# One planned order for the first batch's mixing, and third forms on VectorE, in an RWKV-6 and MLP-mixer kernel

## The chip, the core and the metric

The kernel runs on one core of a Trainium2 chip. The metric is the device time of one execution in microseconds (us). Before the change the median of three runs is 520.51 us (519.77 to 521.84). Five engines work side by side, each on its own queue in order: TensorE (PE; its weight loads are shown as PEld), VectorE (DVE), ScalarE (ACT), GpSimd (POOL) and SyncE (SP), which issues nearly all DMAs here.

## The reference

Four batches, eight heads, 768 tokens, 48 values per head. First a linear attention with a decaying state, then a mixer over tokens and one over channels:

```python
for t in range(S):                                  # attention, per batch and head
    cur = u[:, None] * (k_t outer v_t)
    y[t] = r_t @ (state + cur)
    state = w_t[:, None] * state + (k_t outer v_t)
x = y as (B, 768, 384)
h = relu(x.T @ w_tok1) @ w_tok2                     # 768 -> 256 -> 768 over tokens
u = x + h.T
out = u + relu(u @ w_ch1) @ w_ch2                   # 384 -> 1536 -> 384 over channels
```

The mixer's weights arrive as 64-bit floats and are turned into 32-bit floats on the chip.

## The kernel before

**Attention** is done in twelve units, three per batch (`UB = 3`), each for 256 tokens of a batch; `unit(i)` returns its steps. In the order of their dependence: `ends` (a scan on DVE, L392, and a reciprocal), `keys` (L397), `begins` (a scan, L400), `queries` (L403), `tokens` (transposes on PE, L307) with two copies on ACT (`copied`, L308), `carry` (PE, L323), four pairs of `scaled` on ACT (L458) and `updates` on DVE (L468) that follow each other, `gram` (PE, L277) and `mask` (DVE), `before` (the across product on PE, L337, which needs the fourth `scaled`), `seen` (a small read on ACT, L349), `after` (the within product on PE, L358) and three copies `taken` into x (ACT, L364). Units 0 to 3 compute the term with u by a gram of its own (`own_u` on ACT, `own_gram`, `own_put`); later units by three products on DVE (L420, L422, L425; in the code `products`, the buffer `near`). Two range checks on ACT (`ranges`, L384) read each unit's `to_end`, a buffer that the next unit's `ends` overwrites. `load_rk`, `load_w`, `load_v` and `load_near` issue the loads of the next unit on SP.

**Conversion** of weights goes by pairs of blocks: two loads (L226), on DVE `exponent` (L229), `mantissa` (L235), `add` (L241) and `put` (L244 and two of L247), on ACT `raise_two` (L232) and `signs` (L238). The token weights take three pairs, the channel weights nine (`to_ch`, pairs 0 to 8): `w_ch1` lies in pairs 0 to 4 and `w_ch2` in 4 to 8.

**Mixing of batch 0** is done in 32-bit float: `hidden` (L774), `back` (L781, an addition into x on DVE), `turn` (L789, transposes; a copy on ACT), `up` (L799; three steps and a ReLU on ACT, L802), `down` (L810) for two of three thirds of the tokens (each 12 blocks of hidden channels, `jt`), and `quarters` for the last third: seven products p1 to p7 (L829, L834) of sums of blocks, for which `weight_sum` forms sums of weights on DVE (L764). Blocks `jt` 0 to 3 of `up` need pairs 0 and 1, 4 to 7 pairs 1 and 2, 8 to 11 pairs 3 and 4; of `down`, 0 to 3 need pairs 4 and 5, 4 to 7 pairs 6 and 7, 8 to 11 pairs 7 and 8.

**Mixing of batches 1 to 3** (`exact_mixing`) splits both factors in parts of fewer bits. For the weights `splits(kind, n)` makes three forms, six times for each of the two kinds: up part (ACT, L528), remainder (DVE, L532), low part (ACT, L536), a store of the low part to DRAM (SP, L542 or L544), and the third form "joint" (POOL, L547), the difference of up and low part. Each block then takes `joint` (L624), `ends` (L647, L649), sums and forms of z on ACT, DVE and POOL, and `down` (L661 to L663); the stored low parts come back through a ring of ten slots (`load_third`, L563).

**Order.** `strict` ties the instructions of PE, DVE, ACT and SP to the order in which they are recorded. The attention of batch b + 1 runs beside the mixing of batch b. Up to unit 2 the order is written out by hand. For batch 0's mixing the program has a hand-written list (`ahead`) and then `woven`, which merges lists in proportion to rough weights: conversions with ups, then the rest. For batches 1 and 2 `interleaved` plans: each piece lists its engines, their times and the pieces that it needs, and a small model of the engines' clocks and of the six PSUM banks decides whether the next piece of mixing or of attention is recorded. Batch 1's forms of the second kind (`late`) are set in by hand, two steps at a piece.

```python
pieces = woven(first, woven(both[2:], sum(to_ch[2:8], [])) + woven(downs[0][:4], to_ch[8]))
...
pieces += woven([(0.4, f) for f in e2["ranges"]] + second + sum((a + b for a, b in rest), []), mixed)
```

Of the kernel before, what the change touches and what calls it, by code (L numbers as in the profile page):

```python
# [21 lines left out]
DM = H * D  # L22
# [27 lines left out]

def woven(*lists):

    keyed = []
    for n, pieces in enumerate(lists):
        total, at = sum(c for c, _ in pieces), 0.0
        for i, (c, f) in enumerate(pieces):
            keyed.append(((at + c / 2) / total, n, i, c, f))
            at += c
    return [(c, f) for *_, c, f in sorted(keyed, key=lambda e: e[:3])]


def emit(pieces):
    for _, f in pieces:
        f()
# [3 lines left out]
def rwkv6_then_mixer(  # L68
# [456 lines left out]
    def splits(kind, n):  # L525
# [8 lines left out]
        def low_part():  # L534
            low = formed[kind, n] = slot("z_more", 3, 2) if kind and n % 2 else slot("ring2", 0, 2)
            act.mul(low, form_of(kind, n, "joint").bitcast(f32), -BASE)  # L536
# [9 lines left out]
        def joined():  # L546
            pool.tensor_sub(form_of(kind, n, "joint"), form_of(kind, n, "up").bitcast(f32), formed.pop((kind, n)).bitcast(f32))  # L547

        return [up_part, rest, low_part, store, joined]
# [28 lines left out]
    def exact_mixing(bt):  # L578
# [111 lines left out]
        def add_down(s, half, n, jts):  # L690
            last = jts[-1] % HALF == HALF - 1
            add(("down", s, half, n, jts[-1]), lambda: down(s, half, n, jts), ("PE", 0.525 * len(jts), d(*[("z", s, j) for j in jts]), *([f"a{n}", f"b{n}"] if jts[0] % HALF == 0 else ())),
                *([("DVE", 0.56, ()), ("free", f"a{n}"), ("DVE", 0.56, ()), ("free", f"b{n}")] if last else ()))

        late = []
        if bt == 1:
            for n in range(HALF):
                fs = splits(1, n)
                late += [((bt, "late", n, m), fs[m], ops) for m, ops in enumerate(((("ACT", 0.85, ()),), (("DVE", 0.95, d(("late", n, 0))),), (("ACT", 0.85, d(("late", n, 1))),), (),
                                                                                      (("POOL", 2.2, d(("late", n, 2))),))) if m or n > 1]  # L700
        for i in range(2):
            for c in range(C):
                pieces += [late.pop(0) for _ in range(2 if late else 0)]
                add(("hidden", i, c), lambda i=i, c=c: hidden(i, c), ("PE", 0.65, (), *(["h"] if c == 0 else ())), *([("ACT", 0.49, ()), ("free", "h")] if c == C - 1 else ()))
        if bt == 1:
            add("first", lambda: first_loads(4))
        for c in range(C):
            pieces += [late.pop(0) for _ in range(min(2, len(late)))]
# [3 lines left out]
        if bt == 1:  # L712
            add("second", lambda: first_loads(6))
        for s in range(2):
            for half in range(2):
# [6 lines left out]
                def add_high(jt):  # L722
                    add(("high", s, jt), lambda jt=jt: high_of(jt), ("ACT", 0.49, d(("sum", s, jt))))
# [4 lines left out]
                for jt in jts:  # L728
# [3 lines left out]
                    add(("ends", s, jt), lambda s=s, half=half, jt=jt: end_passes(s, half, jt), ("PE", 1.05, d(*[("turn", s, c) for c in range(3)]), f"a{jt}"))  # L732
# [33 lines left out]
    def mixing(bt, x_of, out_rows):  # L766
# [50 lines left out]
        def quarters(s):  # L817
            z = now["z"][1].rearrange("p (j t) -> p j t", j=NJ)
            a11, a12, a21, a22 = (z[:, ts(j, HALF), ts(i, 128)] for i in range(2) for j in range(2))
            t1, t2, t4, t7 = (w_sum(n) for n in range(4))  # L820
# [4 lines left out]
            def begin(p):  # L825
                a, b = of[p]
# [4 lines left out]
            def rest(p):  # L831
                a, b = of[p]
# [44 lines left out]

            of = {p1: (a11, w11), p4: (a22, t4), p2: (a12, w21), p5: (a22, t1), p7: (a21, t7), p6: (a22, t2), p3: (a11, w22)}
            return [e for p in of for e in ((0.98, lambda p=p: begin(p)), (0.98, lambda p=p: (rest(p), p())))]

        hiddens = [[(0.65, lambda i=i, c=c: hidden(i, c)) for c in range(C)] for i in range(DTOK // 128)]
        backs = [(1.3, lambda c=c: back(c)) for c in range(C)]
        turned = [backs[0]]
        for c in range(1, C):
            turned += [backs[c], (0.3, lambda c=c: turn(c - 1))]
        turned.append((0.3, lambda: turn(C - 1)))
        ups = [[(0.9, lambda s=s: up(s, 0, (0, 1))), (0.4, lambda s=s: up(s, 0, (2,)))] + [(1.3, lambda s=s, jt=jt: up(s, jt)) for jt in range(1, NJ)]
               for s in range(S // SEG)]
        plain = lambda s: [(1.3, lambda n=n, jt=jt: down(s, n, range(jt, jt + 2))) for jt in range(0, NJ, 2) for n in range(2)]
        downs = [plain(s) if s < 2 or bt is None else None for s in range(S // SEG)] + [quarters]  # L890
        return hiddens, turned, ups, downs
# [6 lines left out]
    def steps(i):  # L898

        e = unit(i)  # L900
        up, by = e["updates"], e["scaled"]
        by_tokens = i > UB
        sums = e["products"] if by_tokens else [lambda: None] * 3
        some = lambda fs, c: [(c, f) for f in fs]
        loads, ranges, copied = (0.1, lambda: load_rk(i + 1)), (0.4, e["ranges"][0]), some(e["copied"], 0.2)
        next_w, next_v = (0.1, lambda: load_w(i + 1)), (0.1, lambda: load_v(i + 1))
        ends, keys, begins, tokens, queries = ((c, e[n]) for c, n in ((2.4, "ends"), (1.2, "keys"), (2.2, "begins"), (1.0, "tokens"), (1.2, "queries")))
        if by_tokens:
            first = [loads, ends, keys, ranges, begins, tokens, *copied, queries, next_w]
        else:  # L910
            first = [loads, *some(e["own_u"], 0.2), ends, keys, begins, tokens, *copied]
        second = [] if by_tokens else [(1.0, e["own_gram"]), (1.3, e["own_put"]), (0.1, lambda: sp.dma_start(u_rows, u_all)), ranges, queries, next_w]
        return first, [*second, (0.3, by[0]),
                (1.0, sums[0]), (1.0, e["carry"]), (1.0, sums[1]),
                (0.7, up[0]), (0.3, by[1]), (1.4, e["gram"]), (1.0, sums[2]), (0.1, lambda: load_near(i + 1)),
                (0.7, up[1]), (0.3, by[2]), (1.2, e["mask"]), (0.7, up[2]), (0.3, by[3]),
                *([(1.3, e["sums_put"])] if by_tokens else []), (0.7, up[3]),
                (1.0, e["before"]), (0.1, e["seen"]), (1.5, e["ranges"][1]), (1.0, e["after"]), next_v, *some(e["taken"], 0.3)]

    def attention_pieces(i):  # L920
# [4 lines left out]
        last = lambda *names: tuple((i - 1, n) for n in names)  # L925

        def piece(f, name, *ops):
            return (i, name), f, ops

        return [piece(lambda: load_rk(i + 1), "loads"),  # L930
                piece(e["ends"], "ends", ("DVE", 2.6, last("small", "large"))),
                piece(e["keys"], "keys", ("DVE", 1.25, k("ends"))),
                piece(e["ranges"][0], "small", ("ACT", 1.4, k("ends"))),
                piece(e["begins"], "begins", ("DVE", 2.35, k("ends"))),
                piece(e["tokens"], "tokens", ("PE", 0.9, k("keys"), "k0", "k1")),
                *[piece(e["copied"][n], f"copied{n}", ("ACT", 0.6, k("tokens")), ("free", f"k{n}")) for n in range(2)],
# [4 lines left out]
                piece(e["ranges"][1], "large", ("ACT", 1.4, k("ends"))),  # L941
                piece(up[0], "up0", ("DVE", 0.35, k("carry", "by0"))),
                piece(by[1], "by1", ("ACT", 1.3, k("up0"))),
                piece(sums[0], "sums0", ("DVE", 0.95, ())),
                piece(e["gram"], "gram", ("PE", 1.15, k("keys", "queries"), "g0", "g1")),
                piece(sums[1], "sums1", ("DVE", 0.95, k("sums0"))),
# [3 lines left out]
                piece(sums[2], "sums2", ("DVE", 0.95, k("sums1"))),  # L950
# [3 lines left out]
                piece(e["sums_put"], "put", ("DVE", 1.35, k("sums2", "mask"))),  # L954
# [3 lines left out]
                piece(e["after"], "after", ("PE", 1.15, k("put", "seen"))),  # L958
# [5 lines left out]
    def interleaved(mix, more, room=0.6, hurry=0.04):  # L964

        at = {e: 0.0 for e in ("PE", "DVE", "ACT", "POOL")}
        done, banks, held, out = {}, [0.0] * 6, {}, []
        weigh = lambda pieces: [sum(o[1] for o in ops if o[0] == "PE" or pieces is more and o[0] == "DVE") for _, _, ops in pieces]
        mix, more = list(mix), list(more)
        w_mix, w_more = weigh(mix), weigh(more)  # L970
        total_mix, total_more = sum(w_mix), sum(w_more)
        so_far = [0.0, 0.0]

        def run(piece, really):
            key, f, ops = piece
            clock = at if really else dict(at)
            free = banks if really else list(banks)
            kept = held if really else dict(held)
            delay, end = 0.0, 0.0
            for op in ops:  # L980
                if op[0] == "free":
                    free.append(end + 0.1)
                    kept.pop((key[0], op[1]), None)
                    continue
                engine, t, needs, *takes = op
                ready = max([done.get(n, 0.0) + 0.15 for n in needs], default=0.0)
                if takes:
                    free.sort()
                    for name in takes:
# [246 lines left out]
```

## Time and profile before

| | |
|---|---|
| runs | 520.51 us median (519.77 to 521.84) |
| profiled execution | 521.7 us, of which the span is 520.0 |
| PE busy | 480.2 us (92%) |
| DVE busy | 390.4 us (75%) |
| ACT busy | 267.2 us (51%) |
| POOL busy | 74.0 us (14%) |
| mean granted PE clock | 0.97 |

The span runs from the first to the last instruction. In the profile's slices (40 of 13 us) a digit is the busy share in tenths. `PEclk` is the clock granted to TensorE, in tenths of full speed. A line such as "PE h_ps L605 <- ACT h L600: 8.6, 2, 6.3" says who waited for whom: total us, how often, longest. In the order of time a line has its start, its duration, engine, line, operation, output <- input, shapes, count, and in brackets the idle time ahead of it with what ended it.

In this execution batch 0's `hidden` and `back` reach the first `up` at 61.2 us; ups go on to about 92, downs to 133, the last third's ups to 156, quarters to 182; batch 1's mixing starts at 182.0 and its first `joint` at 213.2.

### The profile page before, as it was taken

The page shows a single profiled execution, that of the slowest core. Times are in us where ns is not written, and L with a number is a line of the kernel's source. Part 1 is how long each engine was busy: PE and PEld are TensorE (multiplying, and loading weights), DVE is VectorE, ACT ScalarE, POOL GpSimd, SP SyncE. Part 2 cuts the span into 40 slices and gives each one's busy share as a digit, 9 for nine tenths or more (in the row PEclk, how much of TensorE's full clock was granted, in tenths as well). Part 3 has the DMA queues.
Part 4 walks back from the last instruction along what each step waited for, and adds up shares of the span by engine and source line. Part 5 has one row for each costly group of instructions (what it writes and reads, how often), then busy time and mean ns, then how long its engine had stood idle before and what let it go on. Part 6 is the DMA issues. An engine that isn't in the chain of part 4 may idle for free.

```text
span 520.0 us, 12857 instructions
## 1 busy us (share of the span) xinstructions
PE 480.2 (92%) x5254; PEld 412.7 (79%) x5254; DVE 390.4 (75%) x591; ACT 267.2 (51%) x632; POOL 74.0 (14%) x70
## 2 busy tenths in 40 slices
PE   3678999999996975999999999999999999999995
PEld 3565788666676933899899976999899967999995
DVE  7999879947689656888889794788887816566552
ACT  3867676635583345537464633637356423353350
POOL 0000000001250044022030300303030200230330
PEclk9699999999998985999999999999999999999998
DMA  8845955247563174448375773357545451254331
GB/s 309 317 160 163 263 167 169 82 127 263 148 189 86 69 206 151 148 154 244 112 235 136 243 254 97 118 172 197 170 145 156 134 184 30 82 162 137 96 121 49
DMA packets 48977, 83.78 MB, mean 161 GB/s; under 512 B 4816, under 2 KB 40272, under 8 KB 48912
## 3 DMA queue, kind: packets, MB, share of 16 engines
q1 hardware_dynamic: 48768, 82.90, 50.9%
q8 instruction: 43, 0.70, 0.6%
q14 instruction: 22, 0.18, 0.1%
q10 hardware_dynamic: 144, 0.00, 0.0%
HBM read 71.87 MB, written 11.01 MB: 159 GB/s over the span
## 4 chain that ended last, share of the span: by engine, by line
PE 58%; DVE 2%; ACT 0%; issue 0%; DVEq 0%
PE joint_ps L624 8%; PE o_ps L661 7%; PE ends_ps L647 7%; PE ends_ps L649 7%; PE o_ps L663 7%; PE o_ps L662 7%; PE h_ps L605 5%; PE h_ps L598 3%; PE y_ps L358 1%; PE gram L277 1%; PE y_ps L337 1%; PE kv_ps L323 1%; PE k_ps L307 1%; PE xT_ps L611 1%; DVE x L671 1%; DVE x L670 1%
## 5 line engine op out<-in xcount | busy, mean ns | idle before, releaser
L635 DVE TENSOR_TENSOR ends_ps<-ends_ps,mid 128x384 f32<-128x384 f32 x72 | 40.6, 564 | 34.7 <-PE ends_ps L649 20.7
L625 ACT ACTIVATE mid<-joint_ps 128x384 f32<-128x384 f32 x72 | 35.1, 487 | 55.2 <-PE joint_ps L624 53.6
L458 ACT ACTIVATE before<-state,to_end 112x48 f32<-112x48 f32 x148 | 37.3, 326 | 47.0 <-DVE state L468 45.4
L624 PE MATMUL joint_ps<-z_more,forms 128*128 128x384 f32 x216 | 51.5, 346 | 0.8 <-DVE z_more L573 0.8
L661 PE MATMUL o_ps<-forms,z_high 128*128 128x384 f32 x144 | 50.1, 348 | 0.0
L647 PE MATMUL ends_ps<-x_forms,forms 128*128 128x384 f32 x216 | 49.4, 336 | 0.0
L649 PE MATMUL ends_ps<-x_forms,ring 128*128 128x384 f32 x216 | 49.3, 337 | 0.0
L799 PE MATMUL z_ps<-xT,wch 128*128 128x256 f32 x216 | 48.4, 381 | 0.6 <-ACT z L802 0.6
L662 PE MATMUL o_ps<-ring,z_high 128*128 128x384 f32 x144 | 48.6, 337 | 0.0
L663 PE MATMUL o_ps<-forms,z_high 128*128 128x384 f32 x144 | 48.4, 336 | 0.0
L799 PEld LDWEIGHTS z_ps<-xT,wch 128*128 128x128 f32 x216 | 40.4, 190 | 6.6 <-ACT z L802 1.0
L576 POOL TENSOR_TENSOR z_more<-z_more 128x384 fp32r<-128x384 f32 x12 | 12.2, 1016 | 233.5 <-DVE z_more L639 111.1
L547 POOL TENSOR_TENSOR forms<-forms,ring 128x768 fp32r<-128x768 f32 x9 | 17.9, 1987 | 175.1 <-DMA rk<-in_rk_dram 123.3
L624 PEld LDWEIGHTS joint_ps<-z_more,forms 128*128 128x128 f32 x216 | 38.4, 188 | 2.4 <-DVE z_more L573 1.1
L647 PEld LDWEIGHTS ends_ps<-x_forms,forms 128*128 128x128 f32 x216 | 38.6, 188 | 0.2
L649 PEld LDWEIGHTS ends_ps<-x_forms,ring 128*128 128x128 f32 x216 | 38.5, 188 | 0.0
L670 DVE SCALAR_TENSOR_TENSOR x<-o_ps,x 128x384 f32<-128x384 f32 x36 | 19.9, 554 | 22.2 <-PE o_ps L662 21.9
L810 PE MATMUL h_ps<-wch,z 128*128 128x384 f32 x96 | 33.1, 493 | 0.0
L661 PEld LDWEIGHTS o_ps<-forms,z_high 128*128 128x128 f32 x144 | 27.0, 188 | 0.8
L631 ACT ACTIVATE z_high<-ends_ps 128x384 fp32r<-128x384 f32 x48 | 23.4, 488 | 7.8 <-DVE ends_ps L635 7.8
L662 PEld LDWEIGHTS o_ps<-ring,z_high 128*128 128x128 f32 x144 | 27.1, 188 | 0.0
L663 PEld LDWEIGHTS o_ps<-forms,z_high 128*128 128x128 f32 x144 | 27.0, 188 | 0.0
(186 smaller groups left out, 1038.9 us busy)
## 6 DMA issues: line engine op xcount, KB each, us to landing
ring<-third SPq DMA_DIRECT2D x144, 192.0 KB, 3.3
raw<-in_w_ch_dram SPq DMA_DIRECT2D x16, 512.0 KB, 4.8
rk<-in_rk_dram SPq DMA_DIRECT2D x36, 192.0 KB, 5.4
near<-in_near_dram SPq DMA_DIRECT2D x8, 768.0 KB, 4.4
w<-in_w_dram SPq DMA_DIRECT2D x10, 520.5 KB, 4.7
vt<-in_v_dram SPq DMA_DIRECT2D x12, 384.0 KB, 4.2
out_dram<-x SPq DMA_DIRECT2D x18, 192.0 KB, 3.0
raw<-in_w_tok_dram SPq DMA_DIRECT2D x6, 512.0 KB, 10.2
```

The source lines that it names most:

```text
L458: act.mul(t[:ROWS, a], state[bt, g][:ROWS, a], by_last(c, j)[:, a:a + 1])
L605: pe.matmul(ps, tok2[:, i, ts(c, 128)], h1[:, i, :], start=(i == 0), stop=(i == DTOK // 128 - 1))
L624: pe.matmul(b, joint[m], xf[2][:, m], start=m == 0, stop=m == 2)
L625: act.mul(mid(jt), b, BASE / (BASE - 1.0))
L635: dve.tensor_add(a, a, mid(jt))
L647: pe.matmul(a, up[m], xf[0][:, m], start=m == 0, stop=False)
L649: pe.matmul(a, low[:, m], xf[1][:, m], start=False, stop=m == 2)
L661: pe.matmul(a, z[0], up, start=first, stop=False, skip_group_check=True)
L662: pe.matmul(a, z[1], held[bt, s, half, 1, jt], start=False, stop=last, skip_group_check=True)
L663: pe.matmul(b, z[2], joint, start=first, stop=last, skip_group_check=True)
L799: pe.matmul(ps, now["wch1"][:, m, ts(jt, 128)], xT[:, m, ts(s, SEG)], start=(m == 0), stop=(m == DM // 128 - 1))
L810: pe.matmul(ps, zs[s][:, jt, ts(n, 128)], now["wch2"][:, jt, :], start=(jt == 0), stop=(jt == NJ - 1))
```

## The change

`woven`, `steps` and the hand-written list `ahead` go. Batch 0's mixing becomes a list of pieces with times and needs (`first_mixing`), unit 3 gets pieces in `attention_pieces` (with its own gram), and `weights_in_turn` is a third stream: conversions, range checks of units 1 and 2, the two copies `kept`, the forms of the first kind, two up parts of the second, and the weights' sums. `interleaved` takes any number of streams: the first sets the pace, another is taken if its next piece has all that it needs recorded, does not run ahead of the first by more than `ahead`, and would not hold its engine up; its clocks and banks go on from batch to batch. DMAs are pieces of a pretended engine "Q" that has no clock. Batch 1's late forms are a stream too. The third form is computed by DVE in place of POOL, and the low parts of the second kind use two slots of `z_more` (the first one `ring2`).

```diff
         def low_part():
-            low = formed[kind, n] = slot("z_more", 3, 2) if kind and n % 2 else slot("ring2", 0, 2)
+            low = formed[kind, n] = slot("z_more", 3 + 2 * (n % 2), 2) if kind and n else slot("ring2", 0, 2)
...
         def joined():
-            pool.tensor_sub(form_of(kind, n, "joint"), form_of(kind, n, "up").bitcast(f32), formed.pop((kind, n)).bitcast(f32))
-
-        return [up_part, rest, low_part, store, joined]
+            dve.tensor_sub(form_of(kind, n, "joint"), form_of(kind, n, "up").bitcast(f32), formed.pop((kind, n)).bitcast(f32))
+
+        back = 2 if kind else 1
+        behind = ((("form", kind, n - back, "store"), ("form", kind, n - back, "joint")) if n >= back else ()) + ((("form", 0, HALF - 1, "joint"),) if kind else ())
...
+                (at("low")[0], low_part, (("ACT", 0.85, at("rest") + behind),)),
+                (at("store")[0], store, (("Q", 4.0, at("low")),)),
+                (at("joint")[0], joined, (("DVE", 0.95, at("low")),))]
...
+    def interleaved(mix, *others, room=0.6, hurry=0.04, ahead=(-0.01, -1.0)):
...
+        def wanted(n):
+            piece = streams[n][0]
+            if not ready(piece):
+                return False
+            engines = [o[0] for o in piece[2] if o[0] != "free"]
+            if not streams[0]:
+                return True
+            lag = spent[0] / totals[0] - spent[n] / totals[n]
+            if lag <= ahead[n - 1]:
+                return False
+            held_up = run(streams[0][0], False) if ready(streams[0][0]) else 1e8
+            if "PE" in engines:
+                stall = run(piece, False)
+                return stall <= 0.05 or stall < held_up - 0.2 or lag > hurry and stall <= held_up + 0.3
+            return not engines or engines[0] == "Q" or clock[engines[0]] - clock["PE"] <= room + (0.8 if lag > hurry else 0.0)
+
+        while any(streams):
+            order = sorted((n for n in range(1, len(streams)) if streams[n]), key=lambda n: spent[n] / totals[n])
+            n = next((n for n in order if wanted(n)), 0)
...
     def single(steps, n):
...
+        whole = [("load", load, ("Q", 5.0, last(2, "add", "signs"))), ("signs", signs, ("ACT", 1.15, k("load") + last(2, "put"))),
+                 ("exponent", exponent, ("DVE", 0.69, k("load") + last(1, "two"))), ("two", raise_two, ("ACT", 1.15, k("exponent") + last(1, "put"))),
+                 ("mantissa", mantissa, ("DVE", 0.69, k("load") + last(1, "put"))), ("add", add, ("DVE", 1.23, k("mantissa"))),
+                 ("put", put, ("DVE", 2.06, k("two", "add", "signs")))]
...
+    def weights_in_turn():
+
+        first = [e for n in range(len(to_ch)) for e in single(to_ch[n], n)]
+        stored = [(("kept", i), lambda i=i: sp.dma_start(kept[i], (wtok1, wtok2)[i].rearrange("p c k -> p (c k)")), ()) for i in range(2)]
+        ranges = [(("of", n), f, (("ACT", 1.4, ()),)) for n, f in enumerate((e1["ranges"][1], *e2["ranges"]))]
+        formed = [e for n in range(HALF) for e in splits(0, n)]
+        sums = [(("sum", n), lambda n=n: weight_sum(n), (("DVE", 1.3, (("down", 0, 1, NJ - 2),) if n < 2 else (("up", 2, NJ - 1, 2),)),)) for n in range(4)]
+        return first[:1] + ranges + first[1:] + stored + formed + [splits(1, n)[0] for n in range(2)] + sums
...
         if bt == 0:
...
+            pieces = interleaved(first_mixing(), attention[1], weights_in_turn())
         elif bt < B - 1:
-            pieces = middle_mixing(bt)
+            rooms.setdefault("mid", mpool.tile([128, 2 * DM], f32, name="mid", tag="o", bufs=1))
+            late = [e for n in range(HALF) for e in splits(1, n)[int(n < 2):]] if bt == 1 else []
+            pieces = interleaved(exact_mixing(bt), attention[bt + 1], *([late] if late else []))
```

## The prediction

> **What bounds the kernel now.** I read the slices of the page first, then busy time by stretches of 13 us, then TensorE's waits, then the order of time in the stretch that the change rewrites. Columns of the stretches: from:to, length, busy time (instructions) of PE, PEld, DVE, ACT, POOL, granted clock, DMA share, GB/s.
>
> ```profile
> PE   3678999999996975999999999999999999999995
> DVE  7999879947689656888889794788887816566552
> PEclk9699999999998985999999999999999999999998
> ```
> ```profile
> 52.00:65.00 13.00, 12.97 (x57) 9.12 (x58) 11.70 (x20) 8.75 (x13) 0.00 (x0) 1.00 0.94 263
> ...
> 104.00:117.00 13.00, 13.00 (x206) 8.13 (x204) 5.34 (x11) 4.60 (x16) 0.00 (x0) 1.00 0.44 127
> ...
> 156.00:169.00 13.00, 8.88 (x141) 7.92 (x140) 11.97 (x13) 5.01 (x15) 0.12 (x1) 0.87 0.31 86
> ...
> 182.00:195.00 13.00, 9.73 (x29) 5.05 (x27) 7.26 (x8) 5.29 (x9) 6.11 (x3) 0.89 0.73 206
> 195.00:208.00 13.00, 7.65 (x25) 5.15 (x26) 8.93 (x8) 6.79 (x11) 5.42 (x3) 0.59 0.45 151
> ```
> ```profile
> PE h_ps L605 <- ACT h L600: 8.6, 2, 6.3
> ...
> PE q_ps L829 <- DVE late_sums L764: 4.1, 1, 4.1
> ```
>
> TensorE is the bound: from 52 us on it idles only at 130 to 169 (6.1 us: 0.95 + 0.87 + 4.12 and crumbs) and 182 to 208 (8.6), 14.7 us in all. The first hole waits for the sums of weights, the second, at the start of batch 1, for a ReLU that stands on ScalarE behind the third forms. After 208 us there is next to nothing to win, and up to 52 us the two programs issue the same order. DVE is nearly full until 104 us and half idle from there to 117: today all conversion of the channel weights (last L247 at 102.9) is done before most of batch 1's attention.
>
> TensorE also pays after a hole:
>
> ```profile
> 192.40:194.10 1.70, 1.61 (x2) 0.50 0.63 231
> 194.10:200.30 6.20, 0.00 (x0) 0.50 0.20 75
> 200.30:203.00 2.70, 2.65 (x4) 0.50 0.98 311
> ```
>
> Here the columns are PE busy, clock, DMA share, GB/s. At half clock for 1.7, 5.5 (200.3 to 205.8) and, after the 4.1 us hole, 3.4 us, it lost half of that: 5.3 us. Today's holes so cost 14.7 + 5.3 = 20.0 us. That is the whole prize.
>
> **The change, part by part.** The prices of a conversion are read here (one pair of blocks, DVE and ACT):
>
> ```profile
> 78.18 0.63 DVE L229 TENSOR_SCALAR raw<-raw 128x1024 uint16<-128x1024 uint16 x1
> 78.73 0.68 DVE L235 TENSOR_SCALAR raw<-raw 128x1024 uint32<-128x1024 uint32 x1
> 78.85 1.15 ACT L232 ACTIVATE raw<-raw,rebias 128x1024 uint16<-128x1024 uint16 x1 [3.44 <-DVE raw L229]
> 79.44 1.23 DVE L241 SCALAR_TENSOR_TENSOR raw<-raw 128x1024 f32<-128x1024 uint32 x1
> 80.58 0.68 DVE L244 TENSOR_TENSOR raw<-raw,first 128x1024 bf16<-128x1024 bf16 x1
> 80.69 1.17 ACT L238 ACTIVATE first<-raw 128x1024 bf16<-128x1024 int32 x1
> 81.30 1.29 DVE L247 SCALAR_TENSOR_TENSOR wch<-raw 128x512 f32<-128x512 f32 x2
> ```
>
> From start to start: exponent 0.6, mantissa 0.65, add 1.15, put 1.95, so 4.35 us of DVE for a pair. Other prices from rows of the same stretch: scans (ends, begins) 2.6 and 2.3, keys and queries 1.2, mask 1.3, a state update 0.35, each of the three product steps 0.95, an addition into x 0.55; ACT's scaling 1.0, range check 1.35; TensorE: an up 1.3, a down of two blocks 1.36, tokens 1.0, carry 1.15, gram 1.15, back 1.38, a turn 0.4.
>
> The work is the same; what changes is the order in which each engine must take it. Batch 1's attention (units 3, 4, 5) now runs among the conversions, and each engine is first in, first out. I followed the four orders of the changed program from the point where they part: TensorE 52.0, DVE 53.2 (end of the L241 at 51.95), ACT 55.2 (end of the range check at 53.94).
>
> Second pair (ups, first step). On ACT unit 3's four products (2.0) and unit 1's second range check (1.35) come first, so ends can start at 58.5. Then DVE has ends 2.6, three additions 1.7, exponent 0.6, keys 1.2, mantissa 0.65, add 1.15, begins 2.3, put 1.95: 70.65. TensorE has six backs 8.3, six turns 2.4, two first ups 1.8, tokens 1.0: 13.5, done at 65.5. It waits 5.2.
>
> Pairs 2 to 4. Unit 3's first gram ends at 76.6 and DVE stands still for it; from there its put 1.3, add 1.15, queries 1.2, pair 2's put 1.95 end at 82.2, TensorE is there at 81.7 (0.5). Gram of unit 3 ends at 91.2: mask 1.3, pair 3's put 1.95, update 0.35, scaling 1.0 give 95.8, TensorE two ups later is at 93.8 (2.0). Then 0.2 for the read behind pair 4's signs, and pair 4's put at 95.8 + 0.35 + 4.35 = 100.5 for a TensorE free at 98.5 (2.0). Together 4.7. The load of pair 3 also stands on SP behind unit 4's w, which waits for queries; it lands near 86, covered. Without that cover each us late is a us more.
>
> First down. Pair 5's power of two stands on ACT behind the ReLU of the last up: 0.5 + 1.15 + put 1.95 = 3.6 of wait, whatever came before.
>
> Third pair of downs. It needs pair 7. DVE's order is: update (after carry on TensorE), two products, update, mask, mantissa, add, third product, update, put: 0.35 + 1.9 + 0.35 + 1.3 + 0.65 + 1.15 + 0.95 + 0.35 + 1.95 = 8.95 from the end of carry. TensorE has only a gram (1.15 + 0.3) there: 7.5 of wait.
>
> Last downs. Pair 8's load stands on SP behind unit 5's near rows, which wait for unit 4's third product (about 129.5): issue 1.5, landing 4.8 (page), 4.35 of DVE end at 140.2, and the three transfers together may take 1 more; TensorE is there at 131.7 + 5.4 = 137.1. Wait 3 to 4; I take 3. (The next wait on SP or ACT that could follow, unit 4's read behind third form 3, is ready in time: four low parts 5.5 apart from 141.2 on end at 158.5, TensorE asks at 159.1.)
>
> Quarters. Batch 1's across product of unit 5 stands on TensorE right after p5; DVE must do p5's 0.95 + 0.95 + 0.55, an update 0.35, ACT 1.0: 4.2 with the semaphores' 0.4, then 0.6 for the last weight sum. 4.8.
>
> Start of batch 1. ReLU 0.6, queries 0.9. Unit 6's across product is moved up in front of the first ends: from queries on DVE has 0.35 + 0.95 + third form 0.95 + remainder 0.95 + 0.95 + 0.35 + 1.3 + 0.95 + 0.35 = 7.1 and ACT 1.0, TensorE 2.0 of work: 6.1 (I use 6.0). Its within product waits for a read that stands on ACT behind three forms' low parts: from the scaling on, 8.0 against TensorE's 3.2: 4.8. Together 12.3, so the second hole is not closed.
>
> Third forms on VectorE: 12 subtractions at 0.96 (L532, same shape) in place of 12 at 1.82 on POOL (L547). That is +11.5 on DVE, less what DVE loses to POOL today (a 2.33 scan took 3.97 beside L547 at 125.3), so between -8 and +11.5. Their time inside the waits is counted above; the others lie in DVE's idle time after pair 8 (without it, up to 6 x 0.96). The low parts' other slots (z_more in place of ring2 for the even forms of the second kind) cost nothing: a slot comes round after two forms as the odd ones do today, and ACT's work on the next form covers the store.
>
> Sum: 5.2 + 4.7 + 3.6 + 7.5 + 3.0 + 4.8 + 12.3 = 41.1. Clock: three holes cost 1.8 each today; seven of these are longer than the smallest (2.3), so between 0 and 12.6. The one after 7.5 is swallowed by the wait for pair 8, the last two share one: I take 7.5. Net 41.1 + 7.5 - 20.0 = 28.6. The profiled execution took 521.7 (span 520.0), 1.2 above the median: 521.7 + 28.6 - 1.2 = 549.
>
> A rule speaks against the change too: the Trainium skill (TensorE: Matmul & The Clock Gate, Part 1: The HAM clock gate) says that an idle window of about 3.4 us halves the clock until a busy window has passed. By it the five waits of 3.6 and more cost up to 1.7 each, 8.5 in place of 7.5, and 550 would come out. The trace agrees after 4.1 and 6.3 us, but it shows half clock after a wait of 2.3 too.
>
> **Rivals.** (a) Faster: the planned order brings each put before TensorE asks. Then the first five waits vanish, batch 1's start runs through because no third form waits for POOL, and 4.8 + 1.5 of the quarters stay: 520.5 - 20.0 + 6.3 = 507. It decides from pair 7's put being done 7.5 us earlier. For it: DVE has 24 us of idle time before pair 8. Against: that idle time lies behind TensorE and ACT in a fixed order. (b) Smaller loss: the early waits and the load are hidden (12.9), and the clock costs no more than today: 520.5 + 3.6 + 7.5 + 4.8 + 12.3 + 5.3 - 20.0 = 534. For it: the early sums rest on small differences. (c) Larger: the low parts of batch 0's forms go through one slot, and ACT blocks until each store has landed; today from one to the next took 4.2 to 7.7 us. At 7.7 the fourth is 6.6 later than I have it, the read for unit 4 behind it costs 6, and the clock takes its upper 5 more: 560.
>
> **How the numbers follow.** Forecast 0.80, (a) 0.05, (b) 0.10, (c) 0.05. The likeliest is 549. The range goes from just under (b) to (c): 531 to 562. A measurement of this kernel can't tell less than 0.5% (2.6 us) from no change: faster than that 0.05, within it 0.02 (the lower edge of (b)), slower 0.93.
>
> **What would show it.** Right: the last L247-type put near 140 instead of 103; waits of TensorE's first down on DVE of 3 to 4 us, of a later down of 7 to 8, half clock behind them; batch 0's quarters end near 207 instead of 182; from the middle of batch 1 on the same pace as before. Wrong: TensorE still full from 65 to 130, or batch 1's first ends coming without holes.

## The result and the profile after

The changed kernel takes 551.38 us (median of four runs, 550.99 to 556.15) where the kernel before takes 520.64 us on the same chip (519.77 to 521.84): 1.061 times as long, with a 95% interval of 1.0548 to 1.0671. The profiled execution took 551.17 us, its span is 549.5 us. The forecast was 549. One kernel below (weights first, loads late) was in a slower state in three of its six executions; its ratio and the comparisons with it leave these out.

In the changed program `up` stands on L783, `down` on L794, a pair's loads on L211, exponent L214, power of two L217, put L229 and L232, the across product L322, the within product L343, the sums of weights L748, the quarters L812 and L817. The page's busy times and three rows of its slices (40 of 13.7 us):

```profile
PE 490.1 (89%) x5254; PEld 421.1 (77%) x5254; DVE 393.4 (72%) x603; ACT 268.8 (49%) x632; POOL 50.1 (9%) x58
...
PE   3678798974799979949999999999999999999995
DVE  7998964956576567877878977688789754556563
PEclk9699999787899979968999999999999999999999
```

TensorE has the same 5254 instructions and is busy 490.1 us, 9.9 more than before: the same work partly at a lower clock. The other 19.6 us of the longer span are idle time. Both lie in the first 19 slices, with the low digits of `PEclk` at or behind the holes of `PE`. DVE, at 7 to 9 in its first eight slices before, falls to 6 and 4 in the sixth and seventh already: it waits there with conversions still to do. TensorE's waits, longest groups (total us, times, longest; the gram's wait for rk stands at the start of both programs):

```profile
PE h_ps L794 <- DVE wch L232: 14.7, 3, 7.2
PE y_ps L322 <- ACT before L443: 9.7, 5, 2.4
PE gram L262 <- DMA rk<-in_rk_dram: 8.6, 1, 8.6
PE y_ps L343 <- ACT seen L334: 5.1, 4, 3.7
PE z_ps L783 <- DVE wch L232: 2.7, 1, 2.7
```

Before, the first and the fifth of these groups were not there at all: no `up` or `down` waited for a weight. The chain behind the three waits of 14.7 us, rows picked from the order of time:

```profile
111.95 0.38 ACT L786 ACTIVATE z<-z_ps 128x256 f32<-128x256 f32 x1 [0.70 <-PE z_ps L783]
112.23 1.14 ACT L217 ACTIVATE raw<-raw,rebias 128x1024 uint16<-128x1024 uint16 x1
115.57 1.53 PE L794 MATMUL h_ps<-wch,z 128*128 128x384 f32 x4 [3.65 <-DVE wch L232]
124.74 0.35 DVE L453 TENSOR_TENSOR state<-before,kv_ps 112x192 f32<-112x192 f32 x1 [3.18 <-PE kv_ps L308]
131.16 0.35 SPq L154 DMA_DIRECT2D near<-in_near_dram  x1
131.64 0.93 SPq L211 DMA_DIRECT2D raw<-in_w_ch_dram  x2
132.78 7.73 PE L794 MATMUL h_ps<-wch,z 128*128 128x384 f32 x16 [7.23 <-DVE wch L232]
139.75 0.69 DVE L214 TENSOR_SCALAR raw<-raw 128x1024 uint16<-128x1024 uint16 x1 [6.43 <-DMA raw<-in_w_ch_dram]
142.94 1.29 DVE L232 SCALAR_TENSOR_TENSOR wch<-raw 128x512 f32<-128x512 f32 x2
144.29 12.26 PE L794 MATMUL h_ps<-wch,z 128*128 128x384 f32 x32 [3.78 <-DVE wch L232]
```

Pair 5's power of two runs on ScalarE at 112.23, directly behind the last ReLU (L786, at 111.95), and the first down waits 3.65 us. DVE then stands 3.18 us for the carry of unit 4 at 124.74 and has unit 4's chain ahead of pair 7's put: 7.23 us for the fifth down. The load of pair 8 leaves SP at 131.64, behind unit 5's near rows, and DVE itself waits 6.43 us for it: 3.78 us for the ninth down. The last put's two rows of L232 begin at 142.94, where before they began at 102.23; batch 1's mixing begins at 210.8 in place of 182.2 and its first `joint` at 231.5 in place of 213.2. The mixing of batch 2 begins at 306.9 before and at 336.1 after, 29.2 us apart, as the ends are 29.5 apart: behind batch 1 there is no difference.

What the holes do to the clock, in stretches (PE busy, instructions, granted clock, DMA share, GB/s):

```profile
132.00:135.00 3.00, 2.23 (x4) 0.50 0.93 281
...
144.00:147.00 3.00, 2.71 (x4) 0.55 0.00 0
```

### The profile page after: what moved, and what is told of

Read it like the earlier page. It is cut to its first block, busy times and chain, and to the rows that moved or that the text cites. A ratio compares the mean times of both kernels' runs of the same rounds, so it can differ in the third digit from the quotient of the medians.

```text
span 549.5 us, 12838 instructions
## 1 busy us (share of the span) xinstructions
PE 490.1 (89%) x5254; PEld 421.1 (77%) x5254; DVE 393.4 (72%) x603; ACT 268.8 (49%) x632; POOL 50.1 (9%) x58
## 4 chain that ended last, share of the span: by engine, by line
PE 75%; DVE 15%; ACT 3%; DMA 3%; issue 2%; SPq 0%; DVEq 0%; ACTq 0%
PE o_ps L653 7%; PE joint_ps L616 7%; PE ends_ps L639 7%; PE ends_ps L641 7%; PE o_ps L655 7%; PE o_ps L654 7%; PE z_ps L783 6%; PE h_ps L794 5%; PE h_ps L597 4%; PE h_ps L590 4%; PE y_ps L343 3%; DMA raw<-in_w_ch_dram 2%; PE gram L262 2%; PE kv_ps L308 2%; PE y_ps L322 1%
## 5 line engine op out<-in xcount | busy, mean ns | idle before, releaser
L783 PE MATMUL z_ps<-xT,wch 128*128 128x256 f32 x216 | 51.2, 394 | 4.0 <-DVE wch L232 2.7
L639 PE MATMUL ends_ps<-x_forms,forms 128*128 128x384 f32 x216 | 50.7, 343 | 0.0
L794 PE MATMUL h_ps<-wch,z 128*128 128x384 f32 x96 | 37.3, 548 | 14.7 <-DVE wch L232 14.7
L783 PEld LDWEIGHTS z_ps<-xT,wch 128*128 128x128 f32 x216 | 41.6, 196 | 10.7 <-DVE wch L232 2.9
L794 PEld LDWEIGHTS h_ps<-wch,z 128*128 128x128 f32 x96 | 20.2, 217 | 29.5 <-DVE wch L232 11.8
L639 PEld LDWEIGHTS ends_ps<-x_forms,forms 128*128 128x128 f32 x216 | 39.4, 192 | 0.3
L641 PEld LDWEIGHTS ends_ps<-x_forms,ring 128*128 128x128 f32 x216 | 39.4, 192 | 0.0
L349 ACT COPY x<-y_ps 64x384 f32<-64x384 f32 (+1 forms) x36 | 17.1, 475 | 22.3 <-PE y_ps L343 21.9
L653 PEld LDWEIGHTS o_ps<-forms,z_high 128*128 128x128 f32 x144 | 27.0, 188 | 0.7
## 6 DMA issues: line engine op xcount, KB each, us to landing
raw<-in_w_tok_dram SPq DMA_DIRECT2D x6, 512.0 KB, 10.5
```

What stands on the lines that cost most here:

```text
L639: pe.matmul(a, up[m], xf[0][:, m], start=m == 0, stop=False)
L641: pe.matmul(a, low[:, m], xf[1][:, m], start=False, stop=m == 2)
L653: pe.matmul(a, z[0], up, start=first, stop=False, skip_group_check=True)
L783: pe.matmul(ps, now["wch1"][:, m, ts(jt, 128)], xT[:, m, ts(s, SEG)], start=(m == 0), stop=(m == DM // 128 - 1))
L794: pe.matmul(ps, zs[s][:, jt, ts(n, 128)], now["wch2"][:, jt, :], start=(jt == 0), stop=(jt == NJ - 1))
```

## The experiments

The theory was that of the prediction: the loss is in the order in which DVE, ScalarE and SP take the work that TensorE waits for during the first batch's mixing. All ratios are to the kernel before, run on the same chip beside each kernel, with the 95% interval.

### The two other parts of the change: third forms, and batch 1's order

**Third forms on POOL again, new order kept.**

```diff
-            dve.tensor_sub(form_of(kind, n, "joint"), form_of(kind, n, "up").bitcast(f32), ...)
+            pool.tensor_sub(form_of(kind, n, "joint"), form_of(kind, n, "up").bitcast(f32), ...)
```

> The changed kernel with the twelve third forms back on GpSimd, the order of everything else unchanged. If the order of the streams makes the loss (my theory): 549 to 556 us, the waits of the first, fifth and ninth down on VectorE as they are (3.6, 7.2, 3.8 us). If the third forms load VectorE too much (rival): under 540 us.

Measured: 556.04 us, 1.0639 [1.0596, 1.0682]. The loss stays; the forms on DVE are not its cause. By the medians they help by a few us, but the interval overlaps the changed kernel's.

**Third forms on DVE, old order kept** (the same line, the other way round, in the kernel before).

> The kernel before, with only the third forms moved to VectorE. My theory: 517 to 523 us, a change of under 3 us. The rival that VectorE has no room for them: 526 us or more.

Measured: 519.4 us, 0.9957 [0.9932, 0.9981]: a gain of 0.4%, some 2 us, real but under what I call a change. DVE is busy 392.4 us in place of 390.4, though twelve subtractions of 0.96 us (11.5) were added to it.

**The old order for batch 0, everything else as changed** (`woven`, `steps` and the hand-written lists put back for batch 0; batch 1 planned with its late forms as a stream).

```diff
-            pieces = interleaved(first_mixing(), attention[1], weights_in_turn())
+            pieces = woven(first, woven(both[2:], sum(tc_[2:8], [])) + woven(downs[0][:4], tc_[8]))
...
+            pieces += woven([(0.4, f) for f in e2["ranges"]] + second + sum((a + b for a, b in rest), []), mixed)
```

> The changed kernel, with the old hand-written and woven order for batch 0's mixing; third forms on VectorE and batch 1's planned order stay. If the loss lies in batch 0's order alone: 516 to 524 us, as the old order with forms on VectorE (519.4). If batch 1's planned start costs as well: 526 us or more.

Measured: 520.27 us, 0.9983 [0.9958, 1.0008]. So the whole loss lies in the planned order of batch 0. The planned start of batch 1 alone is neither good nor bad.

### Which of the order's properties costs

**Attention later.** The attention stream may be taken only when it is 0.3 of its length behind the mixing.

```diff
-            pieces = interleaved(first_mixing(), attention[1], weights_in_turn())
+            pieces = interleaved(first_mixing(), attention[1], weights_in_turn(), ahead=(0.3, -1.0))
```

> The changed kernel, with attention held back until the mixing of batch 0 is 0.3 of its work ahead, so that more conversions come first on VectorE. If the conversions' place behind the attention makes the loss: the waits of ups and downs on puts (17.4 us together) fall under 8 us, batch 0's quarters end near 200 instead of 210.8, and the time is 533 to 545 us, since some of it comes back as attention crowded at the end. If the loss is in batch 1's start or in the clock alone: 549 to 553 us.

Measured: 545.9 us, 1.0444 [1.0383, 1.0506], less than a microsecond over the range of the theory. TensorE's waits of that run, from 52 to 330 us:

```profile
PE y_ps L322 <- ACT before L443: 8.6, 8, 2.0
PE k_ps L292 <- issue: 6.7, 3, 3.6
...
PE h_ps L794 <- DVE wch L232: 2.9, 1, 2.9
```

The waits for puts fell from 17.4 us (14.7 + 2.7) to 3.7 (2.9 and 0.8 on an `up`), which confirms that attention stood in the conversions' way. But the time fell by only about 9 us by the ratios, because attention that is late then holds TensorE itself. Batch 1's mixing begins at 196.1 in place of 210.8, 14.7 us sooner, but batch 2's at 330.6 in place of 336.1, only 5.5 sooner. 6.7 us of TensorE's waits stand at the transposes of the keys, where the profile names no releaser ("issue"). The times name it: TensorE starts them at 120.53, 184.21 and 232.37, each 0.1 us after DVE's `keys` (L382) ends (119.26 + 1.16, 182.89 + 1.22, 231.11 + 1.16). They wait for `keys`, which stands behind the unit's late scan.

**Loads early.** The load of pair n goes directly behind the put of pair n - 2, the first place where its buffer is free.

```diff
+        for n in range(3, len(to_ch)):
+            load = next(e for e in first if e[0] == ("to", n, "load"))
+            first.remove(load)
+            first.insert(1 + next(i for i, e in enumerate(first) if e[0] == ("to", n - 2, "put")), load)
```

> The changed kernel, with each weight pair's load recorded one pair earlier, so that it stands on SP ahead of the loads that wait for attention. If SP's order is part of the loss: VectorE's waits for weights (5.2 and 6.4 us) and the wait of the last downs (3.8 us) go, 541 to 548 us. If the loads are hidden anyway: 550 to 553 us.

Measured: 539.24 us, 1.0338 [1.0307, 1.0369]: 12 us better than the changed kernel, more than I expected. TensorE's waits again, and two lines of the order of time:

```profile
PE h_ps L794 <- DVE wch L232: 7.7, 1, 7.7
```
```profile
105.25 1.14 ACT L217 ACTIVATE raw<-raw,rebias 128x1024 uint16<-128x1024 uint16 x1
...
109.95 1.45 PE L794 MATMUL h_ps<-wch,z 128*128 128x384 f32 x4
```

The 7.7 us behind unit 4's chain stay, as they should. But with the ninth down's wait the first down's is gone too: pair 5's power of two now runs at 105.25, 7 us sooner and no longer behind the last ReLU, and the first down starts without a wait. The code says how a load's place can move work on other engines. The planner counts a load as landed 5.0 us behind the place where it is recorded, ScalarE's `signs` of the same pair stands right behind it in the list, and a piece of DVE or ScalarE is taken only while its engine's planned clock is at most 0.6 us (1.4 when its stream lags) ahead of TensorE's. So a load that is recorded late pushes back what stands behind it in the list. This is read from the code; no run tests it by itself.

**Both together.** The two edits above in one kernel.

> Attention held back by 0.3 and loads a pair earlier, both on the changed kernel. If the two parts of the loss are separate: 530 to 536 us (551 less 6 and less 12). If they are one and the same wait: 537 to 541 us.

Measured: 537.99 us, 1.0317 [1.0273, 1.0362], in the range foretold for one and the same wait. In batch 0 they are not the same. No `down` waits for a weight any more and batch 1's mixing begins at 188.1, 22.7 us sooner than in the changed kernel, where late attention alone won 14.7 and early loads alone 12.9 (197.9). Yet batch 2's begins at 323.5, where the loads alone gave 323.0: what late attention won in batch 0 it loses in batch 1 (waits of 7.5 us at across products and 5.2 at keys in the stretch from 52 to 330). Holding back attention is the wrong lever.

**Conversions first.** Loads early, and the steps of a conversion are always asked ahead of attention.

```diff
-            order = sorted((n for n in range(1, len(streams)) if streams[n]), key=lambda n: spent[n] / totals[n])
+            order = sorted((n for n in range(1, len(streams)) if streams[n]), key=lambda n: -1.0 if streams[n][0][0][0] == "to" else spent[n] / totals[n])
```

> Loads a pair earlier, and of the two side streams the conversions always asked first. If what is left of the loss after the early loads is the conversions' place behind attention on VectorE: the wait of the fifth down (7.7 us) falls under 3 us and the time is 528 to 535 us. If not: 537 to 541 us.

Measured: 535.54 us, 1.0278 [1.0242, 1.0313], at the upper edge of the theory's range. The downs' waits fell to 2.7 us, but one new wait took most of that back:

```profile
PE q_ps L812 <- DVE late_sums L748: 11.3, 1, 11.3
```

**Sums as a stream of their own.** The last two sums overwrite the rows that the forms of the first kind read; does the wait come from those forms, or from the sums' place at the end of the list? The sums go into a fourth stream that is asked first, with that need written out.

```diff
-        return first[:1] + ranges + first[1:] + stored + formed + [splits(1, n)[0] for n in range(2)] + sums
+        return first[:1] + ranges + first[1:] + stored + formed + [splits(1, n)[0] for n in range(2)], sums
```

> Conversions first and loads early as before, and the weights' sums as a stream of their own that is asked first; forms stay behind attention. The late sums overwrite the rows that the forms of the first kind still read, so they can't pass those forms. Theory (the 11.3 us wait comes from the forms in front of the sums, not from the sums' own place): the wait stays at 8 us or more and the time at 533 to 538. Rival (the sums' own place at the end of their list is the cause): wait below 4 us, 524 to 531.

Measured: 530.84 us, 1.0185 [1.0147, 1.0223], and the wait is 2.7 us. My theory of this run falls: it was mostly the sums' own place. What is left is again attention, 8.7 us at across and 4.3 at within products in the whole run.

**All of the weights first.** Loads early, and conversions, forms and sums are asked ahead of attention (the edit is shown against the run with the conversions first).

```diff
-... key=lambda n: -1.0 if streams[n][0][0][0] == "to" else spent[n] / totals[n])
+... key=lambda n: -1.0 if streams[n][0][0][0] in ("to", "form", "sum") else spent[n] / totals[n])
```

> The weights' whole stream that was only partly put first in the run before (conversions) is now asked ahead of attention: conversions, forms and sums, with the loads early. Theory (the loss is in the order in which DVE and ACT meet TensorE's demands, and the 11.3 us wait for the late sums, which lie behind the forms of the first kind, is a remainder of the same kind that can be closed): that wait falls below 3 us and the time to 522 to 530. Rival (attention of batch 1 then comes so late that it is what batch 1's start waits for: the loss moves): 532 to 542, with waits of 5 us and more on rows of attention (gram, tokens, across, within) ahead of batch 1's first joint.

Measured: 522.44 us, 1.0025 [0.9994, 1.0055]. The whole loss of 30 us is gone, by the order alone (priorities and the place of the loads): TensorE is busy 480.1 us with the same 5254 instructions, against 480.2 before. Its only waits over 1.3 us in the order of time from 52 us on:

```profile
113.23 5.83 PE L794 MATMUL h_ps<-wch,z 128*128 128x384 f32 x12 [2.68 <-DVE wch L232]
...
214.78 1.33 PE L616 MATMUL joint_ps<-z_more,forms 128*128 128x384 f32 x3 [6.36 <-DVE z_more L631]
```

**All of the weights first, loads late.** The same without the loads' edit.

> Weights asked first (conversions, forms, sums), but each pair's load stays where the changed kernel records it. Theory (order of the streams is the cause, and the loads' place costs only because attention's loads stand ahead of them; with the weights first few of those do): 521 to 527. Rival (the late loads are a cost of their own, the 12 us that the run with early loads alone won back): 530 to 536, with waits of 3 us and more on the weights' blocks behind loads of pairs.

Measured: 536.2 us (the median of the three executions that count; all six lie between 530.84 and 542.33), 1.0214 [1.0157, 1.027]. By the medians the loads' place is worth 14 us here and was worth 12 without the weights first; the weights first are worth 15 alone and 17 with the loads early, and both together 29. The ratios, whose differences are good to about 4 us, give 14 for the loads alone, 21 for the weights first alone and 30 for both. So the two halves of the loss roughly add up; closer than that the runs don't say. My theory of this run, that a late load costs only where attention's loads stand ahead of it, falls, and the rival, a cost of its own, holds, with the time at the upper edge of its range. Its mark is DVE waiting for the load of a pair, and TensorE for DVE:

```profile
115.43 0.69 DVE L214 TENSOR_SCALAR raw<-raw 128x1024 uint16<-128x1024 uint16 x1 [2.30 <-DMA raw<-in_w_ch_dram]
```
```profile
94.48 3.55 PE L783 MATMUL z_ps<-xT,wch 128*128 128x256 f32 x8 [2.61 <-DVE wch L232]
...
119.37 12.05 PE L794 MATMUL h_ps<-wch,z 128*128 128x384 f32 x28 [4.59 <-DVE wch L232]
...
175.01 1.21 PE L812 MATMUL q_ps<-late_sums,z 128*128 128x192 f32 x6 [2.46 <-DVE late_sums L748]
```

Only the wait at 119.37 stands directly behind that load. DVE waited for no load ahead of the two others, so the rest of what a late load costs seems to lie in the order in which the steps behind it are recorded; that is argued, not shown.

**Second forms sooner.** The one large hole left, 6.4 us, stands behind a remainder L517 that DVE takes only after unit 6's scans. The forms of the second kind may now be taken when DVE is up to 4 us further ahead of TensorE than other pieces may.

```diff
-... clock[engines[0]] - clock["PE"] <= room + (0.8 if lag > hurry else 0.0)
+... clock[engines[0]] - clock["PE"] <= room + (4.0 if piece[0][:2] == ("form", 1) else 0.0) + (0.8 if lag > hurry else 0.0)
```

> The run with the weights first and the loads early, and the late forms of the second kind may be taken when DVE is up to 4 us further ahead of TensorE than other pieces may. In that run's profile the one large hole left is 6.4 us at 208 to 215 (TensorE behind z_more L631, behind ScalarE's L623, behind a low part that waits 3.7 us for its slot's store, all because DVE took the last three remainders L517 only from 202.5 on, after unit 6's scans). Theory (an order that DVE meets in time costs nothing): the hole goes, 514 to 519 and faster than the kernel before. Rival (DVE's pieces that are pushed back, unit 6's scans, then hold TensorE up at its keys, tokens or across product by as much): 520 to 525.

Measured: 517.22 us, 0.9907 [0.9875, 0.9939]: 0.9% faster than the kernel before, clear of the noise. Not all of it is the order's: the old order with the forms on DVE had 0.9957, and the two intervals overlap. The page of that run:

```profile
PE 476.8 (93%) x5254; PEld 409.4 (79%) x5254; DVE 392.5 (76%) x603; ACT 269.1 (52%) x632; POOL 49.9 (10%) x58
...
PEclk9699999989999999999999999999999999999998
```

The hole is gone and nothing of its size took its place (the longest wait behind 52 us is 2.68). But TensorE's idle time is nearly the same, 38.6 us against 39.4 in the run with the weights first and the loads early: smaller waits at the start of batch 1 (0.33, 2.07, 1.81 and 1.09) and one of 1.5 in a later batch took the place of the one of 6.4. What fell is TensorE's busy time, from 480.1 to 476.8 at equal work, with the clock at 0.984 in place of 0.974. So 3.3 of the 4.1 us that the span became shorter (519.5 to 515.4) lie in busy time, which fits the clocks: 0.50 from 214.8 to 220 us, behind that run's hole, and 1.00 from 180 to 225 in this one. Of the theory the time and the vanished hole hold, but the order is not free of waits.

### What a hole costs beyond itself

**Dummy products in the holes.** 156 products of 128 columns of the identity into a spare bank, set ahead of the first, fifth and ninth down, of the across products of units 5 and 6 and of the within product of unit 6, so that the clock finds no idle stretch.

```diff
+    def warm(n):
+        b = bank("warm")
+        for _ in range(n):
+            pe.matmul(b[:, :128], ident, ident, start=True, stop=True)
```

> The changed kernel, with 156 products of the identity, 128 columns each (about 20 us of TensorE at 0.13 each), set into the holes ahead of the first, fifth and ninth down, the across products of units 5 and 6 and the within product of unit 6; nothing reads them. If half clock behind the holes is a part of the loss of its own (PE busy grew by 9.9 us with the same instructions): mean granted clock 0.97 or more and 541 to 547 us. If the waits alone set the time: 549 to 553 us.

Measured: 551.35 us, 1.059 [1.0543, 1.0637], as the rival had it. But the order of time shows that the test was badly sized. Each product became two instructions (312 in all), and 100 of them took 11.43 us, so that the dummies took about 36 us in place of the 20 planned:

```profile
124.83 11.43 PE L1041 MATMUL warm<-ident 128*128 128x128 f32 x100
131.38 1.29 DVE L232 SCALAR_TENSOR_TENSOR wch<-raw 128x512 f32<-128x512 f32 x2
136.10 5.33 PE L794 MATMUL h_ps<-wch,z 128*128 128x384 f32 x16
```

The clock is full (the 16 instructions took 5.33 us in place of 7.73), but the dummies last until 136.1 while the put was done at 132.7: the downs start 3.3 us later than without them, 1.1 later at the first down (116.66 against 115.57) and 2.3 at the ninth (146.62 against 144.29). What the clock gave back the overrun took. On the price of the half clock this run is inconclusive. Two pairs of kernels say more. One is the run with the second forms sooner, above, where idle time stayed and the busy time fell by 3.3. The other differs only in the loads: from all weights first with early loads to the same with late ones the span grows by 15.5 us (519.5 to 535.0), of which TensorE's idle time is 7.6 and its busy time 7.9 (480.1 to 488.0) at equal work, with the mean clock at 0.974 and 0.958. In these two executions about half of the loss is the lower clock.

## Why the prediction was right, point by point

The forecast held by its size and by its cause: the order of batch 0's mixing, with the same work. Not all terms of the sum have the size that it gave them.

- **Second pair**: 5.2 foretold, 4.4 measured in three pieces (0.44, 1.29, 2.67).
- **Pairs 2 to 4**: 4.7 foretold, 2.7 measured (1.91 for the foretold 2.0 at unit 3's across product, 0.78 for 0.2 at its read). The waits for the puts of pairs 2 and 4 (0.5 and 2.0) did not come. These early sums rested on small differences, as rival (b) said.
- **First down**: 3.6 foretold, 3.65 measured, and by the named mechanism (power of two behind the ReLU). "Whatever came before" holds for this recorded order only: with early loads the power of two is recorded sooner and the wait vanishes.
- **Third pair of downs**: 7.5 foretold, 7.23 measured. **Last downs**: 3.0 foretold out of 3 to 4, 3.78 measured. Both by the named mechanisms.
- **Quarters**: 4.8 foretold, 3.4 measured (2.42 + 0.95).
- **Start of batch 1**: 12.3 foretold, 8.4 measured. The wait for a ReLU (0.6) did not come, the one for queries was 0.70 for 0.9. I let the whole across product of unit 6 wait for its fourth scaling; in the trace it starts with the blocks whose state is ready, so the wait comes in pieces of 1.96 and 2.00 in place of 6.0. The within product's was 3.73 for 4.8.
- **Sum of waits**: 41.1 foretold, 34.0 measured as TensorE's idle time from 52 to 260 us. Less the 14.7 of before that is 19.3, and the idle time of the whole span grew by 19.6: the list is complete.
- **Clock**: the term that was too small. 7.5 foretold, and 7.5 - 5.3 = 2.2 net; TensorE's busy time grew by 9.9, so by this count the term was about 15, over my upper bound of 12.6. I gave each stretch at half clock the 1.8 us of before. In the trace they follow nearly every hole (not the one of 2.67 us at 69.94, behind which the clock stays at 1.00) and some last longer: batch 1's start, for which I counted one such stretch, runs at 0.50 from 238 to 250.
- The waits were 7.1 too long and the clock's term 7.7 too short: the sum came within 2.4 us of 551.4 by two errors that cancel. That closeness is luck; with one of the two errors alone it would have been off by 5 to 10 us, still inside the range.
- **Third forms on DVE**: 0 put into the sum, with DVE's time between -8 and +11.5. In the old order DVE's busy time rose by 2.0, so what DVE had lost to POOL was worth about 9.5 of it, and the run was some 2 us shorter.
- **Landmarks**: last put 142.9 (near 140), quarters' end 210.8 (near 207), same pace from the middle of batch 1: all as foretold.
- **Load of pair 3** "covered": DVE stood 5.18 us for it, until 86.78, and TensorE did not wait. **Loads as a whole** 3.0: true for single waits, but not for their part in the cause. The prediction followed each wait to the last thing in front of it and so put one wait down to a load; the runs put 12 to 14 us down to where the loads are recorded. A list of waits says what stands last, not which edit removes most of them.
- Rival (a), a planned order in which each put comes in time, was put at 507 and was not what this change does; with other priorities the same planner reached 517.2.

What stays open: the exact price of a half-clock stretch by itself, why some holes bring one and others don't, and by which step of the plan the loads' place works.

## What to carry to other kernels

When work of several in-order engines is put into one planned order, ask for each stream what TensorE waits for first: here weights had to come ahead of attention, though attention was the longer stream, and sharing in proportion cost 30 us with no instruction added. A load takes none of an engine's time in the plan, yet it needs an early place: recording each a pair sooner was worth 12 to 14 us. Test such causes in pairs, each edit alone and both together: two of them roughly added up (12 and 15 us, 29 together); of two others one lost in the next batch what it had won in the first. And look at busy time beside idle time: a large hole that is broken into small ones can shorten the run by the clock, with nearly the same idle time.

## What the runs showed of the hardware

A short hole can bring the half clock: in the run with the weights first and the loads late TensorE waited 2.46 us at 175.0, and the stretch behind it shows 0.58 (PE busy, instructions, granted clock, DMA share, GB/s):

```profile
175.00:182.00 7.00, 6.99 (x124) 0.58 0.25 78
```

It does not always. In the changed kernel TensorE waited 2.67 us at 69.94, and the whole stretch from 65 to 78 us shows 1.00. In the run with the second forms sooner waits of 2.07, 1.81 and 1.09 us between 191 and 202 left it at 1.00 too.

And in the old order moving twelve subtractions from POOL to DVE made DVE busier by 2.0 us where the subtractions alone are 11.5. DVE's other instructions got shorter when POOL had less to do beside them: ten scans (L400) fell from 26.5 to 23.2 us in all, the twelve remainders (L532) from 14.1 to 11.3, and two groups of the products near the diagonal (L430, L422) from 11.9 to 10.5 and from 8.8 to 7.7.
